# Bounds of query, key and value sizes: fewer TensorE instructions in a two-branch attention kernel

## The chip, the core and the metric

The kernel runs on one core of a Trainium2 chip. Five engines work side by side, each through its own queue in program order: TensorE (PE in the profile, with its weight loads as PEld), VectorE (DVE), ScalarE (ACT), GpSimd (POOL) and SyncE (SP, which issues the transfers). They wait for each other by semaphores. The metric is the time of one execution on the device in microseconds; lower is better. Before the change three runs took 1781.36, 1782.36 and 1781.55 us, median 1781.55.

## The reference

Two attention branches over 2048 positions and 1024 features with 32 heads of 32, their outputs side by side. Branch A works in four segments of 512 positions: inside a segment causal softmax attention, plus a memory of the segments before, mixed by a gate per head. Branch B is linear attention with learned feature maps (two softmaxes a head).

```python
for s in range(N):                      # branch A, N = 4 segments of L = 512
    qs, ks, vs = q[:, :, s], k[:, :, s], v[:, :, s]
    logits = jnp.einsum("bhqd,bhkd->bhqk", qs, ks) * scale + mask
    a_dot = jnp.einsum("bhqk,bhkd->bhqd", _softmax(logits, axis=-1), vs)
    pq = phi(qs)                        # phi(t) = t + 1 where t > 0, else exp(t)
    num = jnp.einsum("bhld,bhde->bhle", pq, M)
    den = jnp.einsum("bhld,bhd->bhl", pq, z)[..., None] + 1e-6
    outs.append(g * num / den + (1.0 - g) * a_dot)
    pk = phi(ks)
    M = M + jnp.einsum("bhld,bhle->bhde", pk, vs)
    z = z + jnp.einsum("bhld->bhd", pk)
# branch A returns o @ wo; branch B: softmax feature maps of q and k,
# kv = phi_k^T v, out = (phi_q kv) / (phi_q z) @ wo; the result is [a, b]
```

All arrays are float32.

## The kernel before

**Precision.** Large products run in float16 in two halves: a float32 matrix is scaled to a known size, rounded to a high half, and the rest becomes the low half; three matmuls (high-high, high-low, low-high) then make one product. The scaling needs a bound for each product's result, so that it too can be split into halves. A bound comes from two sums: for a segment x of the input, `xam[:, x]` holds per partition the largest absolute values, and for a block of weights `wgb[:, k, m]` (queries m = 0, keys m = 1 of group k) or `wvb[:, k]` (values) the sums of absolute values per partition. Their product summed over the 128 partitions bounds every entry of the projection.

**Work.** A group g (eight of them) is four heads, 128 columns of queries and of keys; values come in four blocks of two groups. The order of branch A is a list of 32 units, each one segment and one group: units 0 to 15 take segments 0 and 1 through all groups, units 16 to 31 segments 2 and 3. The index k of the bounds counts groups over both passes: k = 0 to 7 are the groups with segments 0 and 1, k = 8 to 15 the same groups with segments 2 and 3. For the values k = 0 to 3 and 4 to 7. `produce(u)` projects queries, keys and values of a unit, `attend(u)` does its attention, `values(u)` the value projection. `fold` and the `xpair` and `strassen` helpers belong to branch B, whose weights are prepared during branch A.

**The bounds.** `bounds(k, segs, prio)` (line 651) makes, for one group and one or two segments, a tile `bd` of five rows: scale and negative scale, inverse scale, the bound itself and the factor of the exponent. For each segment PE multiplies the column `xam[:, x]`, spread over 128 columns as the weights, with the group's two columns of `wgb` (line 659). DVE then scales and clamps the result (line 662), takes the reciprocal (664) and the exponent's factor (665), and POOL does three small products (667, 670, 671). `bounds_v(k, segs, prio)` (line 673) does the same for a block of values with one column (line 680), with lines 683, 685 and 687 on DVE and 689 on POOL; line 687 also keeps the largest bound of all values in `big`. Readers are `produce` (lines 721 to 734), `values` (700, 707) and `attend` (808, 810, 871).

**When they are called.** Groups 0 and 1 and value block 0 are called with one segment at a time, since segment 1 is loaded later. In the loop over units, every even unit u loads the weights of group u / 2 + 2 and calls its bounds with both segments; every fourth unit (u = 1, 5, ...) does so for the next block of values.

**Order.** Nothing is issued directly. `op(engine, duration, function, r=, w=, prio=)` records an operation with the tiles that it reads and writes, an assumed duration and a priority (twice the unit's number, plus an offset). `Graph.run` then hands out all operations by a simulation: at each step the engine that can start first takes, among those ready, the one with the lowest priority number; for PE those come first whose inputs are safe by a margin. Its choice is the program order of each engine. PSUM banks are given out in the same pass, by kind; the bounds use the kind "misc". Buffers with a tag rotate: a new one may be written when the readers of the one that many buffers before are done (`bd` has four, `bv` three).

Of the kernel before, what the change touches and what calls it, by code (L numbers as in the profile page):

```python
# [8 lines left out]
F32 = mybir.dt.float32  # L9
# [3 lines left out]
AF = mybir.ActivationFunctionType  # L13
# [230 lines left out]
def tile_kernel(ctx: ExitStack, tc: tile.TileContext, ax, aw, awv, awo, beta, bx, bwqk, bwv, bphi, bwo, out):  # L244
# [51 lines left out]
    big = const.tile([128, 2], F32, name="big")  # L296
    nc.vector.memset(big, 0.0)
    wsc = const.tile([128, 3, 2, 2], F32, name="wsc")
    osc2 = const.tile([128, 2, 2], F32, name="osc2")
# [287 lines left out]
    def group(u):  # L587
        return units[u][0] // 2 * NG + units[u][1]
# [7 lines left out]
    bigs, swfs, wscs, oscs, phss = (G.fixed(t) for t in (big, swf, wsc, osc2, phs))  # L596
    pstb, wmb = (G.fixed(t) for t in (pst, wm))
    osc = G.fixed(oa_d)
# [52 lines left out]
    def bounds(k, segs, prio):  # L651


        bd = bds.get(k) or bds.setdefault(k, G.buf("a", [128, 5, 2, 2], F32, "bd", 4))
        s0, n, kk = segs[0], len(segs), k % NG
        v, w = slice(s0 % 2, s0 % 2 + n), [(bd, x % 2) for x in segs]
        ps = bank("misc", [128, 2, 2], "bounds")
        for x in segs:
            op(PE, 0.14, lambda x=x: nc.tensor.matmul(
                ps()[:, x % 2], xam[:, x:x + 1].to_broadcast([128, 128]), wgb[:, kk], start=True, stop=True),  # L660
               r=[(xams, x), (wgbs, (kk, 0)), (wgbs, (kk, 1))], w=[ps], prio=prio)
        op(DVE, 0.1, lambda: nc.vector.tensor_scalar(bd()[:, 3, v], ps()[:, v], 2.0 ** -12, 1e-30, op0=OP.mult, op1=OP.max),
           r=[ps], w=w, prio=prio)
        op(DVE, 0.12, lambda: nc.vector.reciprocal(bd()[:, 2, v], bd()[:, 3, v]), w=w, prio=prio)
        op(DVE, 0.1, lambda: nc.vector.scalar_tensor_tensor(
            bd()[:, 4, v, 0], bd()[:, 3, v, 0], SCALE, bd()[:, 3, v, 1], op0=OP.mult, op1=OP.mult), w=w, prio=prio)
        op(POOL, 0.2, lambda: nc.gpsimd.tensor_tensor(
            bd()[:, 0, v], xsc[:, s0:s0 + n, 0:1].to_broadcast([128, n, 2]), wgs[:, kk, :, 0][:, None, :].to_broadcast([128, n, 2]), op=OP.mult),
           r=[*((xscs, x) for x in segs), (wgss, (kk, 0)), (wgss, (kk, 1))], w=w, prio=prio)
        op(POOL, 0.2, lambda: nc.gpsimd.tensor_tensor(bd()[:, 2, v], bd()[:, 2, v], bd()[:, 0, v], op=OP.mult), w=w, prio=prio)  # L670
        op(POOL, 0.2, lambda: nc.gpsimd.tensor_scalar(bd()[:, 1, v], bd()[:, 0, v], -1.0, None, op0=OP.mult), w=w, prio=prio)

    def bounds_v(k, segs, prio):

        bv = bvs.get(k) or bvs.setdefault(k, G.buf("a", [128, 3, 2], F32, "bv", 3))
        s0, n, kk = segs[0], len(segs), k % 4
        v, w = slice(s0 % 2, s0 % 2 + n), [(bv, x % 2) for x in segs]
        ps = bank("misc", [128, 2], "bounds")
        for x in segs:
            op(PE, 0.14, lambda x=x: nc.tensor.matmul(  # L680
                ps()[:, x % 2:x % 2 + 1], xam[:, x:x + 1].to_broadcast([128, 128]), wvb[:, kk:kk + 1], start=True, stop=True),
               r=[(xams, x), (wvbs, kk)], w=[ps], prio=prio)
# [3 lines left out]
        a, b = s0 % 2, (s0 + n - 1) % 2  # L686
        op(DVE, 0.1, lambda: nc.vector.scalar_tensor_tensor(
            big[:, 0:1], bv()[:, 1, a:a + 1], bv()[:, 1, b:b + 1], big[:, 0:1], op0=OP.max, op1=OP.max), r=w, w=[(bigs, 0)], prio=prio)
        op(POOL, 0.4, lambda: nc.gpsimd.tensor_scalar(bv()[:, 0, v], xsc[:, s0:s0 + n, 0], wvs[:, kk, 0:1], None, op0=OP.mult),
           r=[*((xscs, x) for x in segs), (wvss, kk)], w=w, prio=prio)  # L690

    def values(u):

        s, g = units[u]
        k = group(u) // 2
        w, x, P, d = wt[k, "v"], xt[s], 2 * u, un[u]
        d["bv"] = bv = bvs[k]
        i2, n0, vf = s % 2, 128 * (g % 2), vfb[u % 3]
        sc = d["sc"] = G.buf("a", [128, 4], F32, "sc", 4)
        op(POOL, 0.39, lambda: nc.gpsimd.tensor_scalar(sc(), gate1[:, 4 * g:4 * g + 4], bv()[:, 1, i2:i2 + 1], None, op0=OP.mult),  # L700
           r=[gates, (bv, i2)], w=[sc], prio=P + VPRIO)
# [5 lines left out]
        op(ACT, 0.62, lambda: nc.scalar.activation(vf()[:, :, 0:128], ps(), AF.Copy, scale=bv()[:, 0, i2:i2 + 1]),  # L707
           r=[ps, (bv, i2)], w=[vf], prio=P + VPRIO)

    def produce(u):  # L710
# [3 lines left out]
        d = un.setdefault(u, {})  # L714
        bd, i2, st = bds[k], s % 2, stk[u % 3]
        h3 = d["h3"] = G.buf("slot", [128, 2, 2, 512], F16, "h3", 2)
        for m in (1, 0):
            ps = bank("proj", [128, 512])
            product((ps, ps), lambda a, c: (w, (m, a, c // 4), lambda m=m: w()[:, m, a, c, :]), at(x), NC, P, dur=0.215)
            E = P  # L720
            op(ACT, 0.57, lambda ps=ps, m=m: nc.scalar.activation(h3()[:, m, 0], ps(), AF.Copy, scale=bd()[:, 2, i2, m:m + 1]),
               r=[ps, (bd, i2)], w=[(h3, (m, 0))], prio=E)
            op(DVE, 0.6, lambda ps=ps, m=m: nc.vector.scalar_tensor_tensor(
                h3()[:, m, 1], ps(), bd()[:, 2, i2, m:m + 1], h3()[:, m, 0], op0=OP.mult, op1=OP.subtract),
               r=[ps, (h3, (m, 0)), (bd, i2)], w=[(h3, (m, 1))], prio=E)
# [4 lines left out]
            if (m == 1 and s < NSEG - 1) or (m == 0 and s > 0):  # L730
                d[name] = p = G.buf("a", [128, 512], F32, name, 2)
                z = G.buf("a", [128, 512], F32, "z", 1)
                for o, i in ((z, 0), (p, 1)):
                    op(ACT, 0.59, lambda o=o, i=i, ps=ps, m=m: nc.scalar.activation(o(), ps(), AF.Relu, scale=bd()[:, i, i2, m:m + 1]),
                       r=[ps, (bd, i2)], w=[o], prio=E)
                op(ACT, 0.5, lambda p=p: nc.scalar.activation(p(), p(), AF.Exp, bias=0.0, scale=-1.0), w=[p], prio=E)
                op(POOL, 1.25, lambda p=p, z=z: nc.gpsimd.tensor_tensor(p(), p(), z(), op=OP.add), r=[z, p], w=[p], prio=E)
        values(u)

    def attend(u):  # L740
        s, g = units[u]
        d, P = un.pop(u), 2 * u + 1
        st, vl, vf, bd, bv, i2 = stk[u % 3], vlb[u % 2], vfb[u % 3], bds[group(u)], d["bv"], s % 2
        KR, QR = [(st, (1, r)) for r in range(3)], [(st, (0, r)) for r in range(3)]
# [60 lines left out]
        def v4(t):  # L805
            return t()[:, :, 0:128].rearrange("p c (h d) -> p c h d", d=32)

        act(0.52, lambda: nc.scalar.activation(vl()[:, :, :, 33:65], v4(vf), AF.Copy, scale=bv()[:, 2, i2:i2 + 1]),
            r=[vf, (bv, i2)], w=[(vl, 0)])
        dve(0.6, lambda: nc.vector.scalar_tensor_tensor(  # L810
            vl()[:, :, :, 0:32], v4(vf), bv()[:, 2, i2:i2 + 1], vl()[:, :, :, 33:65], op0=OP.mult, op1=OP.subtract),
            r=[vf, (bv, i2), (vl, 0)], w=[(vl, 1)], port=True)
# [43 lines left out]
        def scores(blocks, diag):  # L856
# [13 lines left out]
            pe(0.218, f, r=KR + QR + [(st, (1, 3))] + [(st, (0, 3 + h)) for h, _ in blocks], w=[ps])  # L870
            act(0.59, lambda: nc.scalar.activation(ps(), ps(), AF.Exp, bias=0.0, scale=bd()[:, 4, i2, 0:1]), r=[(bd, i2)], w=[ps])  # L871
            ph = G.buf("a", [128, 2, 512], F16, "ph", 6)
# [194 lines left out]
    for u in range(NU):  # L1067
# [19 lines left out]
        attend(u)  # L1087
# [485 lines left out]
```

## Time and profile before

| what | value |
|---|---|
| median of three runs | 1781.55 us (1781.36 to 1782.36) |
| span of the profiled execution, the only time that it has | 1779.5 us |
| instructions | 38925 |
| PE busy | 1715.4 us, 96% |
| weight loads busy | 1040.4 us, 58% |
| DVE busy | 1457.1 us, 82% |
| ACT busy | 1130.8 us, 64% |
| POOL busy | 922.3 us, 52% |
| matmul records of line 659 (queries and keys) | 64 |
| matmul records of line 680 (values) | 32 |
| granted TensorE clock, mean | 0.992 |

How to read it: the span is the time from the first to the last instruction on the profiled core, and "busy" sums the time in which an engine worked. A row of a line or tile gives the engine, the operation, what it writes `<-` what it reads, the shapes, and the durations in nanoseconds as least / median / most. A view of waits names who waited, for whom, the total in microseconds, how often and the longest. Matmuls overlap one another, so the duration of one record is longer than the time that it takes from the stream. Branch A, where the bounds are made, ends at about 920 us; what follows is branch B's second half and the output products.

### The profile page before, as it was taken

To read this page: it belongs to the slowest core of one execution; us is meant where nothing else is said; L and a number is where in the kernel's file an instruction comes from. 1 tells how busy PE (TensorE), PEld (TensorE's weight loads), DVE (VectorE), ACT (ScalarE), POOL (GpSimd) and SP (SyncE) were. 2 spreads that over 40 slices of the span, in tenths; PEclk is the share of its full clock that TensorE was granted. 3 is DMA by queue.
4 is the path that set the end of the run, shared out by engine and by line. 5 is a ranking of instruction groups with operands and counts; after the bars stand their busy time and mean duration, and the time that the engine had idled before them with its cause. 6 is when DMAs were issued, how large, how long until landed. Compare 5 with 4: busy or idle time off the path is not lost. (4 is left out here: it accounts for less than half of the span.)

```text
span 1779.5 us, 38925 instructions
## 1 busy us (share of the span) xinstructions
PE 1715.4 (96%) x14712; PEld 1040.4 (58%) x14712; DVE 1457.1 (82%) x3367; ACT 1130.8 (64%) x2095; POOL 922.3 (52%) x1141
## 2 busy tenths in 40 slices
PE   7999999999999999999989989999899999999999
PEld 5767766677776777677644444444555444554444
DVE  6989989899787888788877999988997888877541
ACT  6897886987866878689674756444644454344441
POOL 6445454555756687777583544433456677431000
PEclk9999999999999999999989999999999999999999
DMA  6546555574545453674565244276411333133311
GB/s 208 169 144 183 159 153 158 167 225 129 160 128 156 109 179 110 161 217 121 179 202 193 96 168 137 113 272 227 139 49 63 119 125 107 66 143 137 119 65 65
DMA packets 173260, 258.92 MB, mean 146 GB/s; under 512 B 69904, under 2 KB 122896, under 8 KB 164368
## 3 DMA queue, kind: packets, MB, share of 16 engines
q1 hardware_dynamic: 173072, 256.44, 44.9%
q8 instruction: 115, 1.88, 0.4%
q14 instruction: 73, 0.60, 0.1%
HBM read 145.44 MB, written 85.00 MB: 129 GB/s over the span
## 5 line engine op out<-in xcount | busy, mean ns | idle before, releaser
L359 PE MATMUL proj<-S,S 128*128 128x128 f16 (+1 forms) x3072 | 502.7, 299 | 5.5 <-ACT S L386 3.6
L359 PEld LDWEIGHTS <-S 128*128 128x128 f16 x4608 | 331.3, 99 | 153.6 <-issue 8.9
L549 PE MATMUL proj<-S,S 128*128 128x512 f16 x1488 | 348.7, 382 | 12.3 <-ACT cs L555 3.9
L549 PEld LDWEIGHTS <-S 128*128 128x128 f16 x1968 | 189.0, 99 | 231.3 <-issue 17.2
L880 POOL TENSOR_SCALAR_AFFINE_SELECT ph<-ph 128x256 f16<-128x256 f16 (+1 forms) x448 | 196.3, 460 | 171.8 <-DVE ph L874 134.9
L874 DVE SCALAR_TENSOR_TENSOR ph<-s,ph 128x512 f16<-128x512 f32 x320 | 210.4, 683 | 56.5 <-ACT ph L873 54.5
L775 DVE CUSTOM_DVE_ANT_0 s<-s,causal 128x512 f32<-128x512 f32 (+3 forms) x512 | 242.3, 510 | 12.0 <-PE s L769 8.4
L871 ACT ACTIVATE s<-s,bd 128x512 f32<-128x512 f32 x320 | 212.2, 710 | 21.8 <-PE s L867 21.4
L873 ACT ACTIVATE ph<-s 128x512 f16<-128x512 f32 x320 | 190.4, 656 | 0.6
L1119 ACT ACTIVATE e<-e,sk 128x256 f32<-128x256 f32 x256 | 113.9, 497 | 98.3 <-DVE e L1116 94.5
L359 PE MATMUL misc<-S,ot 128*128 128x512 f16 x768 | 174.1, 379 | 0.0
L1415 POOL TENSOR_TENSOR e<-e,zb 128x512 f32<-128x512 f32 x64 | 84.5, 1343 | 71.5 <-DVE r L1122 65.8
L359 PEld LDWEIGHTS <-ot 128*128 128x128 f16 x768 | 73.4, 98 | 82.1
L769 PE MATMUL s<-S 96*128 96x512 f16 (+3 forms) x512 | 113.3, 300 | 5.8 <-DVE mt L775 4.2
L867 PE MATMUL s<-S 104*128 104x512 f16 (+3 forms) x512 | 113.9, 300 | 1.5 <-DVE quad L1011 0.8
L359 PE MATMUL proj<-wv,S 128*128 128x128 f16 x1536 | 104.2, 221 | 0.3 <-DVE mt L775 0.3
L903 PEld LDWEIGHTS <-ph 128*128 128x128 f16 x2560 | 87.8, 96 | 18.0 <-POOL ph L880 2.0
L1226 POOL TENSOR_TENSOR e<-e,r 128x1024 f32<-128x1024 f32 x32 | 64.4, 2017 | 61.3 <-DVE r L1125 50.4
L903 PE MATMUL pv<-vl,ph 128*128 128x66 f16 (+1 forms) x2560 | 92.9, 185 | 2.2 <-POOL ph L880 1.6
L1122 DVE TENSOR_REDUCE r<-e 128x32 f32<-128x1024 f32 x64 | 76.7, 1205 | 21.6 <-ACT e L1119 21.6
L1428 POOL TENSOR_TENSOR e<-e,r 128x1024 f32<-128x1024 f32 x32 | 62.9, 1970 | 41.9 <-DVE r L1426 38.3
L549 PE MATMUL s<-S,S 128*128 128x512 f16 x324 | 77.1, 379 | 1.8 <-ACT cs L555 1.8
(302 smaller groups left out, 3334.8 us busy)
## 6 DMA issues: line engine op xcount, KB each, us to landing
S<-h SPq DMA_DIRECT2D x192, 128.0 KB
S<-wf_d SPq DMA_DIRECT2D x21, 1024.0 KB
st<-bwqk SPq DMA_DIRECT2D x64, 256.0 KB
wf_d<-fo SPq DMA_DIRECT2D x48, 256.0 KB
out<-os SPq DMA_DIRECT2D x40, 256.0 KB
wf_d<-oT SPq DMA_DIRECT2D x36, 256.0 KB
S<-xf_d SPq DMA_DIRECT2D x9, 1024.0 KB
S<-aw SPq DMA_DIRECT2D x16, 512.0 KB
```

Source lines behind the costliest of these rows:

```text
L359: op(PE, dur, lambda c=c, a=a, b=b, lv=lv, rv=rv: nc.tensor.matmul(pv(), lv(), rv(), start=(c == 0 and a + b == 0), stop=(c == n - 1 and a ...
L549: op(PE, 0.215, lambda n=n, a=a, b=b, lv=lv, rv=rv: nc.tensor.matmul(ps(), lv(), rv(), start=(start and n == 0 and a + b == 0), stop=(n == ...
L769: nc.tensor.matmul(ps()[:, o:o + 128 * i + 128], st()[0:96, 0, h, 128 * i:128 * i + 128], st()[0:96, 1, h, 0:128 * i + 128], start=True, s ...
L775: dve(0.12 + 0.00113 * n, lambda h=h, i=i, o=o, n=n: nc.vector.tensor_tensor_reduce(ps()[:, o:o + n], ps()[:, o:o + n], causal[:, 512 - n: ...
L867: nc.tensor.matmul(ps()[:, o:o + n], st()[0:104, 1, h, 128 * j:128 * j + 128], st()[0:104, 0, h, 128 * j:512], start=True, stop=True)
L871: act(0.59, lambda: nc.scalar.activation(ps(), ps(), AF.Exp, bias=0.0, scale=bd()[:, 4, i2, 0:1]), r=[(bd, i2)], w=[ps])
L873: act(0.5, lambda: nc.scalar.activation(ph()[:, 0], ps(), AF.Copy, scale=2.0 ** 14), r=[ps], w=[(ph, 0)])
L874: dve(0.6, lambda: nc.vector.scalar_tensor_tensor(ph()[:, 1], ps(), 2.0 ** 14, ph()[:, 0], op0=OP.mult, op1=OP.subtract), r=[ps, (ph, 0)], ...
L880: nc.gpsimd.affine_select(pd, pd, pattern=[[0, n], [1, 128]], compare_op=OP.is_ge, fill=0.0, base=0, channel_multiplier=-1)
L903: nc.tensor.matmul(ps()[:, i, n0:n1], ph()[:, a, o:o + 128], vl()[:, j, h, n0:n1], start=(i == 0 and a == 0), stop=(j == min(i, 2)), skip_ ...
L1119: op(ACT, 0.41, lambda i=i: nc.scalar.activation(e()[:, 4 * i:4 * i + 4], e()[:, 4 * i:4 * i + 4], AF.Exp, bias=0.0, scale=sk()[:, i:i + 1 ...
L1415: op(POOL, 1.35, lambda a=a, h0=h0, e=e: nc.gpsimd.tensor_tensor(e()[:, 8 * a:8 * a + 8], e()[:, 8 * a:8 * a + 8], zv()[:, h0:h0 + 8], op= ...
```

## The change

Three edits in `bounds` and `bounds_v`, and one where they are called.

1. For the second pass (k = 8 to 15, values 4 to 7) the bounds of all groups are made by one call, for k = 8 and k = 4. Each segment's matmul then has all columns of `wgb` (16) or `wvb` (4) on its right. One buffer of a new tag (`bdh`, `bvh`) holds them for the whole pass; calls for later k are dropped.
2. In the first pass, where both segments are asked for at once (groups 2 to 7, values 1 to 3), POOL first multiplies `xam` of the two segments with the group's columns into a small tile `pr`, and PE sums that over the partitions with one matmul, whose weights are the column of ones. This takes the place of two matmuls.
3. The rows of `bd` are four instead of five (the bound itself lies in row 1 until POOL overwrites it with the negative scale), the readers index through a small function, and the ring of `bv` has two buffers instead of three. The largest value bound of the second pass is taken by a reduction into a new tile `vmx` and a maximum with `big`, and line 689's product becomes one of two tensors.

The readers in `produce`, `values` and `attend` read the same numbers at new places. The core of the diff:

```diff
     def bounds(k, segs, prio):
-        bd = bds.get(k) or bds.setdefault(k, G.buf("a", [128, 5, 2, 2], F32, "bd", 4))
-        s0, n, kk = segs[0], len(segs), k % NG
-        v, w = slice(s0 % 2, s0 % 2 + n), [(bd, x % 2) for x in segs]
-        ps = bank("misc", [128, 2, 2], "bounds")
-        for x in segs:
-            op(PE, 0.14, lambda x=x: nc.tensor.matmul(
-                ps()[:, x % 2], xam[:, x:x + 1].to_broadcast([128, 128]), wgb[:, kk], start=True, stop=True),
-               r=[(xams, x), (wgbs, (kk, 0)), (wgbs, (kk, 1))], w=[ps], prio=prio)
+        rest = k >= NG
+        ks = slice(0, NG) if rest else slice(k % NG, k % NG + 1)
+        nk = NG if rest else 1
+        if k not in bds:
+            t = G.buf("a", [128, 4, 2, nk, 2], F32, "bdh" if rest else "bd", 1 if rest else 4)
+            for i in range(nk):
+                bds[k + i] = (t, lambda i=i: t()[:, :, :, i, :])
...
+        if n > 1 and not rest:
+            pr = G.buf("a", [128, 2, nk, 2], F32, "pr", 1)
+            op(POOL, 0.2, lambda: nc.gpsimd.tensor_tensor(
+                pr(), xam[:, s0:s0 + n, None, None].to_broadcast(shape), wgb[:, None, ks].to_broadcast(shape), op=OP.mult),
+               r=[(xams, x) for x in segs] + wg, w=[pr], prio=prio)
+            op(PE, 0.14, lambda: nc.tensor.matmul(ps(), one.to_broadcast([128, 128]), pr(), start=True, stop=True),
+               r=[pr], w=[ps], prio=prio)
+        else:
+            for x in segs:
+                op(PE, 0.14, lambda x=x: nc.tensor.matmul(
+                    ps()[:, x % 2], xam[:, x:x + 1].to_broadcast([128, 128]), wgb[:, ks], start=True, stop=True),
+                   r=[(xams, x)] + wg, w=[ps], prio=prio)
...
     def bounds_v(k, segs, prio):
-        bv = bvs.get(k) or bvs.setdefault(k, G.buf("a", [128, 3, 2], F32, "bv", 3))
+        rest = k >= 4
+        ks = slice(0, 4) if rest else slice(k % 4, k % 4 + 1)
+        nk = 4 if rest else 1
+        if k not in bvs:
+            t = G.buf("a", [128, 3, 2, nk], F32, "bvh" if rest else "bv", 1 if rest else 2)
...
+        if n > 1 and not rest:
+            pr = G.buf("a", [128, 2, nk, 1], F32, "pr", 1)
+            op(POOL, 0.2, lambda: nc.gpsimd.tensor_tensor(
+                pr()[:, :, :, 0], xam[:, s0:s0 + n, None].to_broadcast(shape), wvb[:, None, ks].to_broadcast(shape), op=OP.mult),
+               r=[(xams, x) for x in segs] + wv, w=[pr], prio=prio)
+            op(PE, 0.14, lambda: nc.tensor.matmul(ps(), one.to_broadcast([128, 128]), pr()[:, :, :, 0], start=True, stop=True),
+               r=[pr], w=[ps], prio=prio)
...
+        if rest:
+            op(DVE, 0.1, lambda: nc.vector.tensor_reduce(vmx, bv()[:, 1, v], axis=AX.XY, op=OP.max), r=w, w=[vmxs], prio=prio)
+            op(DVE, 0.1, lambda: nc.vector.tensor_tensor(big[:, 0:1], big[:, 0:1], vmx, op=OP.max), r=[vmxs], w=[(bigs, 0)], prio=prio)
...
-            x = 2 * ((u // 4 + 1) // 4)
-            bounds_v(u // 4 + 1, [x, x + 1], 2 * u + 0.5)
+            if u // 4 + 1 <= 4:
+                x = 2 * ((u // 4 + 1) // 4)
+                bounds_v(u // 4 + 1, [x, x + 1], 2 * u + 0.5)
...
-            x = 2 * ((k + 2) // NG)
-            bounds(k + 2, [x, x + 1], 2 * u + 3.5)
+            if k + 2 <= NG:
+                x = 2 * ((k + 2) // NG)
+                bounds(k + 2, [x, x + 1], 2 * u + 3.5)
```

More of the change, by code (lines that the diff above doesn't have):

```diff
@@ L297, in tile_kernel @@
     nc.vector.memset(big, 0.0)
+    vmx = const.tile([128, 1], F32, name="vmx")
     wsc = const.tile([128, 3, 2, 2], F32, name="wsc")
@@ L596, in tile_kernel @@
     bigs, swfs, wscs, oscs, phss = (G.fixed(t) for t in (big, swf, wsc, osc2, phs))
-    pstb, wmb = (G.fixed(t) for t in (pst, wm))
+    pstb, wmb, vmxs = (G.fixed(t) for t in (pst, wm, vmx))
     osc = G.fixed(oa_d)
@@ new lines, in bounds @@
+        v, w, shape = slice(s0 % 2, s0 % 2 + n), [(bd, x % 2) for x in segs], [128, n, nk, 2]
+        ps = bank("misc", [128, 2, nk, 2], "bounds")
+        wg = [(wgbs, (i, m)) for i in range(ks.start, ks.stop) for m in range(2)]
+        if n > 1 and not rest:
[10 more added lines that the diff above has]
+                   r=[(xams, x)] + wg, w=[ps], prio=prio)
@@ L667, in bounds @@
         op(POOL, 0.2, lambda: nc.gpsimd.tensor_tensor(
-            bd()[:, 0, v], xsc[:, s0:s0 + n, 0:1].to_broadcast([128, n, 2]), wgs[:, kk, :, 0][:, None, :].to_broadcast([128, n, 2]), op=OP.mult),
-           r=[*((xscs, x) for x in segs), (wgss, (kk, 0)), (wgss, (kk, 1))], w=w, prio=prio)
+            bd()[:, 0, v], xsc[:, s0:s0 + n, 0][:, :, None, None].to_broadcast(shape),
+            wgs[:, ks, :, 0][:, None].to_broadcast(shape), op=OP.mult),
+           r=[*((xscs, x) for x in segs), *((wgss, (i, m)) for i in range(ks.start, ks.stop) for m in range(2))], w=w, prio=prio)
@@ L673, in bounds_v @@
     def bounds_v(k, segs, prio):
-        bv = bvs.get(k) or bvs.setdefault(k, G.buf("a", [128, 3, 2], F32, "bv", 3))
[L676 to L682, printed above, removed]
+        rest = k >= 4
[3 more added lines that the diff above has]
+            t = G.buf("a", [128, 3, 2, nk], F32, "bvh" if rest else "bv", 1 if rest else 2)
+            for i in range(nk):
+                bvs[k + i] = (t, lambda i=i: t()[:, :, :, i])
+        bv = bvs[k][0]
+        s0, n = segs[0], len(segs)
+        v, w, shape = slice(s0 % 2, s0 % 2 + n), [(bv, x % 2) for x in segs], [128, n, nk]
+        ps = bank("misc", [128, 2, nk], "bounds")
+        wv = [(wvbs, i) for i in range(ks.start, ks.stop)]
+        if n > 1 and not rest:
[5 more added lines that the diff above has]
+               r=[pr], w=[ps], prio=prio)
+        else:
+            for x in segs:
+                op(PE, 0.14, lambda x=x: nc.tensor.matmul(
+                    ps()[:, x % 2], xam[:, x:x + 1].to_broadcast([128, 128]), wvb[:, ks], start=True, stop=True),
+                   r=[(xams, x)] + wv, w=[ps], prio=prio)
         op(DVE, 0.1, lambda: nc.vector.tensor_scalar(bv()[:, 1, v], ps()[:, v], 2.0 ** -15, 1e-30, op0=OP.mult, op1=OP.max),
@@ L685, in bounds_v @@
         op(DVE, 0.12, lambda: nc.vector.reciprocal(bv()[:, 2, v], bv()[:, 1, v]), w=w, prio=prio)
[L686 to L690, printed above, removed]
+        if rest:
+            op(DVE, 0.1, lambda: nc.vector.tensor_reduce(vmx, bv()[:, 1, v], axis=AX.XY, op=OP.max), r=w, w=[vmxs], prio=prio)
+            op(DVE, 0.1, lambda: nc.vector.tensor_tensor(big[:, 0:1], big[:, 0:1], vmx, op=OP.max), r=[vmxs], w=[(bigs, 0)], prio=prio)
+        else:
+            a, b = s0 % 2, (s0 + n - 1) % 2
+            op(DVE, 0.1, lambda: nc.vector.scalar_tensor_tensor(
+                big[:, 0:1], bv()[:, 1, a], bv()[:, 1, b], big[:, 0:1], op0=OP.max, op1=OP.max), r=w, w=[(bigs, 0)], prio=prio)
+        op(POOL, 0.4, lambda: nc.gpsimd.tensor_tensor(
+            bv()[:, 0, v], xsc[:, s0:s0 + n, 0][:, :, None].to_broadcast(shape), wvs[:, ks, 0][:, None].to_broadcast(shape), op=OP.mult),
+           r=[*((xscs, x) for x in segs), *((wvss, i) for i in range(ks.start, ks.stop))], w=w, prio=prio)
     def values(u):
```

30 lines of the change are left out of this document (16 added, 14 removed).

## The prediction

> **What bounds the kernel now.** I read the page of the profiled execution first: the busy shares, and the span in forty slices.
>
> ```profile
> span 1779.5 us, 38925 instructions
> PE 1715.4 (96%) x14712; PEld 1040.4 (58%) x14712; DVE 1457.1 (82%) x3367; ACT 1130.8 (64%) x2095; POOL 922.3 (52%) x1141
> PE   7999999999999999999989989999899999999999
> PEclk9999999999999999999989999999999999999999
> ```
>
> TensorE (PE) is busy 96% of the span at almost the full granted clock; VectorE (DVE) comes next with 82%. An average hides stages, so the next view is busy time by stretch (columns: length, then PE, weight loads, DVE, ACT, POOL with their counts, clock, DMA share, GB/s).
>
> ```profile
> 100.00:200.00 100.00, 98.83 (x1090) 71.27 (x1088) 90.28 (x234) 83.64 (x153) 52.45 (x84) 1.00 0.54 165
> 200.00:300.00 100.00, 94.87 (x989) 65.17 (x988) 90.14 (x259) 82.83 (x149) 47.70 (x80) 0.98 0.53 162
> 300.00:400.00 100.00, 97.00 (x1071) 70.91 (x1068) 88.75 (x243) 82.48 (x150) 51.32 (x86) 0.98 0.61 182
> 400.00:500.00 100.00, 99.56 (x1107) 71.06 (x1106) 84.70 (x258) 75.50 (x143) 63.34 (x106) 1.00 0.47 141
> 500.00:600.00 100.00, 100.00 (x1074) 70.13 (x1072) 79.10 (x246) 68.64 (x124) 61.76 (x90) 1.00 0.47 132
> 600.00:700.00 100.00, 99.79 (x1128) 71.56 (x1126) 86.23 (x234) 81.83 (x152) 75.19 (x114) 1.00 0.46 138
> 700.00:800.00 100.00, 99.25 (x1109) 71.01 (x1106) 81.08 (x248) 72.51 (x133) 73.71 (x107) 1.00 0.65 188
> 800.00:900.00 100.00, 97.90 (x1007) 65.92 (x1005) 82.30 (x235) 81.01 (x143) 69.39 (x102) 1.00 0.49 141
> ```
>
> All the work that the change touches lies between 57 and 768 us (rows below). There PE idles 1.17 + 5.13 + 3.00 = 9.3 us from 100 to 400 and 0.44 + 0 + 0.21 + 0.75 + 2.10 = 3.5 us from 400 to 900. Whatever leaves PE's stream there should shorten the stage by nearly its full length, since almost nothing waits for another engine.
>
> Third, the two lines whose matmuls go away, and how they stand in PE's stream (timeline of PE alone: start, length, engine, line, operation, tiles, count).
>
> ```profile
> L659 PE MATMUL misc<-wgb,xam x64: 165/251/251, 16.4 to 765.8; 128*128 128x2 f32 x64
> L680 PE MATMUL misc<-wvb,xam x32: 165/250/250, 27.7 to 711.9; 128*128 128x1 f32 x32
> 57.57 0.36 PE L370 MATMUL misc<-xam,one 128*128 128x1 f32 x2
> 57.84 0.56 PE L659 MATMUL misc<-wgb,xam 128*128 128x2 f32 x4
> 58.26 0.38 PE L359 MATMUL proj<-wv,S 128*128 128x128 f16 x4
> ...
> 71.87 0.38 PE L867 MATMUL s<-S 104*128 104x512 f16 x1
> 72.09 0.50 PE L659 MATMUL misc<-wgb,xam 128*128 128x2 f32 x4
> 72.46 0.38 PE L359 MATMUL proj<-S,S 128*128 128x512 f16 x1
> ...
> 507.25 0.34 PE L659 MATMUL misc<-wgb,xam 128*128 128x2 f32 x2
> 507.45 0.58 PE L680 MATMUL misc<-wvb,xam 128*128 128x1 f32 x4
> 507.89 0.36 PE L659 MATMUL misc<-wgb,xam 128*128 128x2 f32 x2
> 508.12 0.38 PE L359 MATMUL proj<-S,S 128*128 128x512 f16 x1
> ```
>
> Each float32 matmul of the program leaves two records: 32 products of line 659 are 64 records, 16 of line 680 are 32. The 250 ns of one record is not its cost, for they overlap; the cost is the distance to the next start. Two records span 0.36 us, one 0.25, so they start 0.11 us apart. A group of four takes 58.26 - 57.84 = 0.42 us behind narrow products and 72.46 - 72.09 = 0.37 behind a product 512 wide; eight in a row take 508.12 - 507.25 = 0.87.
>
> **The change part by part.** The sum is made on the profiled execution, whose only time is its span, 1779.5 us, 2.05 us under the median of the runs, 1781.55; I take the saving off the median.
>
> (1) Groups 8 to 15 of queries and keys: eight calls of two products become one call of two products, 16 columns wide. Seven calls, 28 records, leave PE. Most stand among narrow products at 0.42 us: 7 x 0.42 = 2.9 us. The remaining call keeps its four records. That 16 columns cost no more than 2 is bounded by a float32 product of 128 columns:
>
> ```profile
> 71.43 0.61 PE L1008 MATMUL misc<-phib,st 128*128 128x128 f32 x4
> L1008 PE MATMUL misc<-phib,st 128*128 128x128 f32 x256 | 36.1, 279 | 0.1
> L1125 DVE RECIPROCAL r<-r 128x32 f32<-128x32 f32 x64 | 21.3, 340 | 0.4
> ```
>
> Four of those span 0.61 us, one 0.28, so (0.61 - 0.28) / 3 = 0.11 us apart, as for 2 columns: nothing is added.
>
> (2) Values 4 to 7: four calls become one; three calls of four records go, 3 x 0.87 / 2 = 1.3 us.
>
> (3) Groups 2 to 7 and values 1 to 3: nine calls with both segments at once. Four records become two, the weights now the column of ones: 9 x 2 x 0.11 = 2.0 us. Single-segment calls (groups 0 and 1, value 0) keep theirs.
>
> Together 28 + 12 + 18 = 58 of 96 records and 2.9 + 1.3 + 2.0 = 6.2 us of PE's stream.
>
> (4) Added: nine small products on POOL, each ahead of PE's matmul, which now waits for POOL instead of for sizes that were long there. The nearest duration is line 667; the nearest wait is the one of the value products for the masked scores.
>
> ```profile
> L667 POOL TENSOR_TENSOR bd<-xsc,wgs x18: 188/200/650, 21.3 to 767.9; 128x4 f32<-128x4 f32 x14, 128x2 f32<-128x2 f32 x4
> L903 PE MATMUL pv<-vl,ph 128*128 128x66 f16 (+1 forms) x2560 | 92.9, 185 | 2.2 <-POOL ph L880 1.6 <-DVE mt L775 0.3 <-DVE ph L874 0.2
> PE pv L903 <- POOL ph L880: 1.6, 4, 0.9
> POOL ph L880 <- PE s L867: 7.9, 4, 4.2
> 87.12 0.65 POOL L667 TENSOR_TENSOR bd<-xsc,wgs 128x4 f32<-128x4 f32 x1
> ```
>
> Nine times 0.2 = 1.8 us of POOL, which is busy 52%. For PE: 2560 / 20 = 128 groups of value products stood behind POOL and lost 1.6 us, 0.0125 each; nine such waits make 0.1 us. The other end is nine times the longest, 0.9, or 8.1 us; below zero nothing speaks for a gain by the wait itself. I take 0.1, because the order puts a product where its inputs are expected, as it does for those 128. Behind a waiting matmul all of PE's stream queues, and then ACT and DVE, which read its banks.
>
> The row of line 667 also shows a spread of 188 to 650 ns. The Trainium skill, "GPSIMD Engine Reference", section "Key points", says that POOL shares its memory interfaces with DVE and contends with DVE instructions of two SBUF inputs; by its rule the added products would take the long end. The trace can't name the cause, but 9 x 0.65 = 5.9 us of POOL would still lie beside PE.
>
> (5) Removed on DVE and POOL, beside PE's work: seven calls' and three calls' worth of six and four small instructions.
>
> ```profile
> L662 DVE TENSOR_SCALAR bd<-misc x18: 145/159/164, 16.8 to 766.1; 128x4 f32<-128x4 f32 x14, 128x2 f32<-128x2 f32 x4
> L664 DVE RECIPROCAL bd<-bd x18: 147/167/178, 17.0 to 767.4; 128x4 f32<-128x4 f32 x14, 128x2 f32<-128x2 f32 x4
> L665 DVE SCALAR_TENSOR_TENSOR bd<-bd x18: 129/148/2053, 17.1 to 767.5; 128x2 f32<-128x2 f32 x14, 128x1 f32<-128x1 f32 x4
> L871 ACT ACTIVATE s<-s,bd x320: 623/690/958, 59.6 to 923.2; 128x512 f32<-128x512 f32 x160
> ```
>
> On DVE 7 x (0.159 + 0.167 + 0.148) = 3.3 us, and some 1.5 more for the values at like durations; the one call that does it all at once works on up to 32 elements, 0.34 us at most by line 1125 instead of 0.17. I cost and credit nothing: in these stretches PE does not wait for DVE beyond the few us above. POOL loses about 5 us and gains 1.8.
>
> (6) Lateness. The bounds of group k are made in unit 2k - 4 and first read in unit 2k. A unit lasts (923.2 - 59.6) / 32 = 27 us by line 871, so four units cover one more small step on POOL, even where POOL came to line 667 at 87.12, 15 us after the matmul at 72.09. The values' ring shrinks from three buffers to two: call k is made in unit 4k - 3 and takes the buffer last read in unit 4k - 5, two units earlier. Nothing waits. No DMA is added, removed or moved past another.
>
> Sum: -6.2 + 0.1 = -6.1 us, 1781.55 - 6.1 = 1775.4.
>
> **The rivals.** First, the order is drawn anew (not slower at its mild end, slower at its hard end). The order on all engines is written by a planner that picks by readiness and priority; from the first changed call, at 72 us, everything may be exchanged with its neighbours. For it: PE's idle share differs fourfold between stretches of the same loop, 9.3 us in 300 (3.1%) against 3.5 in 500 (0.7%), so 400 to 900 has more to lose than to gain. If it idled like 100 to 400, 500 x 9.3 / 300 = 15.5 us, that is 12 more and 1775.4 + 12 = 1787.4. Against: the units around are the same, with fewer small steps between. It ends on the slow side from 6.1 + 3.6 = 9.7 us of new idle time; with half of 12 it gives 1781.4, no change. It may also gain: half of the 9.3 us closed gives 1770.8.
>
> Second, the records were nearly free. Behind the 512-wide product the first of the four costs 0.37 - 3 x 0.11 = 0.04 us, its weight load hidden. Were all so, 58 x 0.04 = 2.3 us, 1779.2, within what a measurement can tell. Against it stand the rows with 0.11 and the 0.87 for eight. The Trainium skill, "TensorE: Matmul & The Clock Gate", section "Back-to-back issue gap", gives 1 to 64 columns about 60 cycles, some 25 ns, as the gap of an isolated matmul; by that an estimate of 58 x 25 ns = 1.5 us, 1780.1. The trace disagrees for float32 records that follow each other, 0.11 us.
>
> Third, PE stands behind POOL. POOL's in-order queue holds masks that themselves wait for score products (4.2 us at the longest). If the nine waits cost the mean of those, 7.9 / 4 = 2.0 each, 18 us are lost and the time is 1781.55 - 6.2 + 18 = 1793; it is slower from 9.8 / 9 = 1.1 us a wait, more than the longest wait of PE for POOL seen, 0.9.
>
> **How the numbers follow.** A run tells about 0.2% from no change, 3.6 us. The saving lands, with small losses or gains of order: 0.60, own range 1770 to 1778. No change: 0.22, of which order 0.18 and free records 0.04. Slower: 0.18, order 0.15 and POOL 0.03. So 0.60, 0.22, 0.18. The range takes in the gaining order at 1770.8, a little more below, and most of the losing one: 1769.5 to 1786, leaving out about one in ten on each side.
>
> **What would show it.** Lines 659 and 680's successors with 24 and 14 records; PE's busy time some 6 us lower, its idle time before 900 us still near 13 us after the first 100; unit starts after 400 us earlier by steps of 0.4; waits of PE on the new product under 1 us in sum. Wrong: PE's idle time up by more than 4 us in 100 to 900 or after 900, a new row "PE misc" waiting for POOL "pr" with a microsecond or more, or PE's busy time down by 2 us only.

## The result, and the profile after

Four runs of the changed kernel took 1773.0 to 1774.87 us, median 1773.51; four of the kernel before took a median of 1781.95 us. The ratio is 0.9941 with a 95% interval from 0.9928 to 0.9953, which is 10.5 us (8.4 to 12.8); the medians lie 8.4 us apart, at the near end of it. The forecast was 1775.4 us, in a range of 1769.5 to 1786.0, and faster as the likeliest case. The profiled execution of the changed kernel spans 1771.4 us against 1779.5.

The page of the changed kernel, busy shares and the granted clock in forty slices:

```profile
span 1771.4 us, 38769 instructions
PE 1711.7 (97%) x14654; PEld 1036.3 (58%) x14654; DVE 1454.1 (82%) x3338; ACT 1133.2 (64%) x2095; POOL 921.8 (52%) x1126
PEclk9999999999999999999989999999999999999999
```

PE has 14712 - 14654 = 58 records fewer, as counted. Its busy time fell by 1715.4 - 1711.7 = 3.7 us only; the other 4.4 us of the span are idle time that went. The two executions differ in the granted clock too, 0.992 before and 0.988 after: 0.004 x 1775 = 7 us of clock were withheld in addition, which by an estimate can hide up to as much of the busy time that the records saved. Busy time by stretch says where (columns as in the prediction: length, PE, weight loads, DVE, ACT, POOL, clock, DMA share, GB/s):

```profile
100.00:200.00 100.00, 100.00 (x1113) 72.37 (x1112) 90.48 (x248) 85.54 (x156) 51.18 (x85) 1.00 0.56 163
200.00:300.00 100.00, 96.99 (x1032) 70.01 (x1029) 94.19 (x263) 86.27 (x155) 51.58 (x87) 0.98 0.58 172
300.00:400.00 100.00, 99.17 (x1083) 70.17 (x1083) 84.85 (x235) 81.95 (x148) 50.14 (x92) 1.00 0.58 174
400.00:500.00 100.00, 98.97 (x1138) 72.15 (x1135) 90.22 (x257) 77.01 (x143) 64.02 (x98) 1.00 0.55 163
500.00:600.00 100.00, 100.00 (x1125) 70.94 (x1124) 83.78 (x239) 79.23 (x145) 71.75 (x101) 1.00 0.51 145
600.00:700.00 100.00, 98.98 (x1115) 69.81 (x1114) 83.20 (x247) 76.42 (x139) 67.31 (x98) 1.00 0.39 120
700.00:800.00 100.00, 98.92 (x1046) 68.77 (x1045) 84.00 (x250) 76.62 (x141) 74.90 (x101) 1.00 0.63 194
800.00:900.00 100.00, 97.92 (x956) 64.41 (x954) 79.99 (x218) 75.01 (x132) 74.00 (x102) 0.97 0.51 146
```

From 100 to 400 us PE idles 0 + 3.01 + 0.83 = 3.8 us where it idled 9.3; from 400 to 900 it idles 5.2 us where it idled 3.5. The sum of the prediction has no term for the 5.5 us that went from 100 to 400: the change removes work from PE, not waits. From 800 to 900 the clock is 0.97 where it was 1.00.

The products for the bounds, by line, in the changed kernel (least / median / most ns, first and last start):

```profile
L669 POOL TENSOR_TENSOR pr<-xam,wgb x6: 196/201/645, 57.1 to 360.4; 128x4 f32<-128x4 f32 x6
L707 POOL TENSOR_TENSOR pr<-xam,wvb x3: 197/197/198, 99.6 to 335.1; 128x2 f32<-128x2 f32 x3
L672 PE MATMUL misc<-pr,one x12: 167/252/272, 72.4 to 362.0; 128*128 128x4 f32 x12
L676 PE MATMUL misc<-wgb,xam x12: 182/251/263, 16.4 to 380.2; 128*128 128x2 f32 x8, 128*128 128x16 f32 x4
L710 PE MATMUL misc<-pr,one x6: 166/251/251, 101.1 to 337.0; 128*128 128x2 f32 x6
L714 PE MATMUL misc<-wvb,xam x8: 167/250/253, 28.0 to 380.8; 128*128 128x1 f32 x4, 128*128 128x4 f32 x4
```

PE's stream around two of them, a timeline of PE alone in the same kernel:

```profile
72.41 0.28 PE L672 MATMUL misc<-pr,one 128*128 128x4 f32 x2
72.55 0.59 PE L360 MATMUL proj<-S,S 128*128 128x512 f16 x2
...
380.15 0.34 PE L676 MATMUL misc<-wgb,xam 128*128 128x16 f32 x2
380.35 0.38 PE L360 MATMUL proj<-S,S 128*128 128x512 f16 x1
```

Lines 672 and 676 hold 24 records, 710 and 714 hold 14, 38 of the former 96. The bounds of group 2 now take 72.55 - 72.41 = 0.14 us of the stream, where four records took 0.37. Two records 16 columns wide take 380.35 - 380.15 = 0.20 us, no more than two of 2 columns took before (507.25 to 507.45). No row of waits names PE as waiting for the product on POOL. The last exponential of branch A, line 910 now, starts earlier by 923.2 - 908.8 = 14.4 us, while the whole span is 8.1 us shorter:

```profile
L910 ACT ACTIVATE s<-s,bdh x160: 640/695/847, 499.0 to 908.8; 128x512 f32<-128x512 f32 x160
```

### The profile page after: what moved, and what is told of

It is laid out like the page before. It is cut to its first block, busy times and chain, and to the rows that moved or that the text cites. A ratio compares the mean times of both kernels' runs of the same rounds, so it can differ in the third digit from the quotient of the medians.

```text
span 1771.4 us, 38769 instructions
## 1 busy us (share of the span) xinstructions
PE 1711.7 (97%) x14654; PEld 1036.3 (58%) x14654; DVE 1454.1 (82%) x3338; ACT 1133.2 (64%) x2095; POOL 921.8 (52%) x1126
## 5 line engine op out<-in xcount | busy, mean ns | idle before, releaser
L550 PE MATMUL proj<-S,S 128*128 128x512 f16 x1488 | 348.9, 383 | 12.8 <-ACT cs L556 6.9
L814 DVE CUSTOM_DVE_ANT_0 s<-s,causal 128x256 f32<-128x256 f32 (+3 forms) x512 | 242.8, 508 | 9.2 <-PE s L808 3.9
L910 ACT ACTIVATE s<-s,bdh 128x512 f32<-128x512 f32 x160 | 106.0, 706 | 17.8 <-PE s L906 17.0
L910 ACT ACTIVATE s<-s,bd 128x512 f32<-128x512 f32 x160 | 107.1, 715 | 13.0 <-PE s L906 7.3
```

Of the source, the lines that this page charges most:

```text
L550: op(PE, 0.215, lambda n=n, a=a, b=b, lv=lv, rv=rv: nc.tensor.matmul(ps(), lv(), rv(), start=(start and n == 0 and a + b == 0), stop=(n == ...
L814: dve(0.12 + 0.00113 * n, lambda h=h, i=i, o=o, n=n: nc.vector.tensor_tensor_reduce(ps()[:, o:o + n], ps()[:, o:o + n], causal[:, 512 - n: ...
```

## The experiments

All comparisons are with the kernel before on the same chip; its median there was between 1783.7 and 1785.3 us. An interval of a ratio is some 0.1% to either side, about 2 us.

### What the records cost, with the order of the work kept

In the kernel before, with the order of the work kept on every engine, one product serves both segments and the second is not issued (shown for `bounds`; `bounds_v` has the same edit):

```diff
+        left = [False, True]
         for x in segs:
-            op(PE, 0.14, lambda x=x: nc.tensor.matmul(
-                ps()[:, x % 2], xam[:, x:x + 1].to_broadcast([128, 128]), wgb[:, kk], start=True, stop=True),
+            op(PE, 0.14, lambda x=x: (nc.tensor.matmul(
+                ps()[:, x % 2], xam[:, x:x + 1].to_broadcast([128, 128]), wgb[:, kk], start=True, stop=True) if n == 1 else
+                nc.tensor.matmul(ps(), xam[:, s0:s0 + 1].to_broadcast([128, 128]),
+                                 wgb[:, kk][:, None, :].to_broadcast([128, 2, 2]), start=True, stop=True) if left.pop() else None),
```

> The kernel before with its order kept on every engine: where both segments are asked for, only one of the two products is issued (to all columns, with the first segment's sizes, so the second segment is scaled by the first one's bound), and the second is left out. 21 products, 42 records, leave PE and nothing else moves. Theory A, a record costs its distance of 0.11 us: 42 x 0.11 = 4.6 us less than before, near 1777.3. Rival B, the order drawn anew made the gain and records are nearly free: 42 x 0.04 = 1.7 us or less, near 1780.3. Rival C, the small DVE and POOL steps that went made it: no change here, since they all stay.

Measured: 1778.63 us, ratio 0.9970 (0.9959 to 0.9982), that is 5.4 us less (3.2 to 7.3) for 42 records. On its page PE's busy time is 1715.4 - 1711.4 = 4.0 us lower, at the same clock of 0.992:

```profile
PE 1711.4 (96%) x14670; PEld 1035.3 (58%) x14670; DVE 1455.7 (82%) x3367; ACT 1131.4 (64%) x2095; POOL 923.0 (52%) x1141
```

The opposite, in the changed kernel with its order kept: the taken records are issued again in place (shown for `bounds`; `bounds_v` has the same edit).

```diff
-            op(PE, 0.14, lambda: nc.tensor.matmul(ps(), one.to_broadcast([128, 128]), pr(), start=True, stop=True),
+            op(PE, 0.14, lambda: [nc.tensor.matmul(ps(), one.to_broadcast([128, 128]), pr(), start=True, stop=True) for _ in range(2)],
...
-                op(PE, 0.14, lambda x=x: nc.tensor.matmul(
+                op(PE, 0.14, lambda x=x: [nc.tensor.matmul(
-                    ps()[:, x % 2], xam[:, x:x + 1].to_broadcast([128, 128]), wgb[:, ks], start=True, stop=True),
+                    ps()[:, x % 2], xam[:, x:x + 1].to_broadcast([128, 128]), wgb[:, ks], start=True, stop=True) for _ in range(nk)],
```

> The changed kernel with its order kept, and every taken record put back in place: the product with ones is issued twice, the second pass's products of queries and keys eight times and those of values four times, 29 products or 58 records more. Theory A: 58 x 0.11 = 6.4 us above the changed kernel, near 1779.9, some 2 us under the kernel before; these 2 us are then what the new order and the steps gone from DVE and POOL are worth. Rival B: little above the changed kernel, 1774 to 1776. Rival C: as B, since the DVE and POOL steps stay away.

Measured: 1780.42 us, ratio 0.9984 (0.9975 to 0.9993). Against the changed kernel's 0.9941 the 58 records cost 0.0043 x 1783 = 7.7 us (some 5 to 10, with the intervals of both ratios). The page of the changed kernel with the records put back:

```profile
span 1780.4 us, 38886 instructions
PE 1720.8 (97%) x14712; PEld 1044.1 (59%) x14712; DVE 1454.1 (82%) x3338; ACT 1133.3 (64%) x2095; POOL 920.7 (52%) x1126
```

In the two profiled executions, both at a clock of 0.988, all of it is PE's busy time: 1720.8 - 1711.7 = 9.1 us, and the span grew by 9.0. Both runs agree with theory A, 5.4 against 4.6 expected and 7.7 against 6.4; over both it is 13.1 / 100 = 0.13 us a record, and the interval of the first, 0.08 to 0.17, holds the 0.11 read from the trace. Rival B (records nearly free) falls, and rival C (only the DVE and POOL steps count) falls as the whole cause. What is left under the kernel before with all records back, 1 - 0.9984 = 2.9 us (1.2 to 4.5), is the worth of the new order and of the steps gone from DVE and POOL together; these two were not told apart.

### One half of the change at a time

The second pass alone: the changed kernel, in which both conditions for the product on POOL are switched off.

```diff
-        if n > 1 and not rest:
+        if False:
```

> The changed kernel without the product on POOL: in the first pass two products on PE as before, in the second one call for all groups. 40 records fewer than before, on PE 40 x 0.11 = 4.4 us. Theory A with a new order worth about what it was in the full change: 1775 to 1778. Rival B, order decides: anything from 1770 to 1786, not in step with the records. Rival C, the DVE and POOL steps that go (all of them go here) bring the gain: 1773 to 1775, as the full change.

The first pass alone: no call for all groups (shown for `bounds`; `bounds_v` has the same edit). Both halves keep the other parts of the change, the four rows of `bd` and the ring of two for `bv`.

```diff
-        rest = k >= NG
+        rest, later = False, k >= NG
...
-        if n > 1 and not rest:
+        if n > 1 and not later:
...
-            if k + 2 <= NG:
+            if True:
```

> The kernel before with the product on POOL and one product on PE in the first pass alone; the second pass makes its bounds call by call, with two products each. 18 records fewer than before, 18 x 0.11 = 2.0 us. Theory A with an order effect of a few us: 1778 to 1781. Rival B: anything from 1770 to 1786. Rival C: no gain, as no DVE step goes and POOL has nine more: 1781 to 1783. The sum of the losses of this one and of the second pass alone against the full change's 8.4 us tells how far the parts add up.

Measured: the second pass alone, with 40 records fewer, 1783.97 us, ratio 1.0005 (0.9996 to 1.0014): no gain. The first pass alone, with 18 fewer, 1771.76 us, ratio 0.9931 (0.9919 to 0.9944): as fast as the whole change. The parts go against the count of the records. With the cost measured above (0.13 us each) the second half saved some 5 us on PE and lost as much elsewhere, and the first saved 2.3 and gained some 10 elsewhere. Both expectations of theory A with a mild effect of order missed, and so did rival C for both; only "order decides" held. The pages, the second pass alone and then the first alone:

```profile
PE 1716.8 (96%) x14672; PEld 1038.6 (58%) x14672; DVE 1450.9 (81%) x3338; ACT 1133.6 (64%) x2095; POOL 916.3 (51%) x1117
PE 1709.4 (97%) x14694; PEld 1037.3 (59%) x14694; DVE 1453.4 (82%) x3367; ACT 1131.8 (64%) x2095; POOL 923.5 (52%) x1150
```

The second pass alone has 40 records fewer than before and yet 1.4 us more of PE's busy time. The granted clock differs: 0.9876 in the mean of its runs, 0.9934 in those of the first pass alone, 0.9899 in those of before. By an estimate the second half had 0.0023 x 1784 = 4.1 us of clock withheld more than before and the first 0.0035 x 1772 = 6.2 less, so a good part of what the halves lost and gained elsewhere is clock and not idle time. Busy time by stretch of the second pass alone, and then of the first alone:

```profile
100.00:400.00 300.00, 290.54 (x3140) 206.95 (x3139) 269.20 (x735) 248.22 (x448) 150.50 (x249) 0.99 0.56 169
400.00:900.00 500.00, 496.27 (x5417) 348.33 (x5416) 415.42 (x1209) 384.16 (x697) 341.05 (x496) 0.99 0.51 149
900.00:1400.00 500.00, 467.29 (x3143) 236.58 (x3142) 432.52 (x739) 267.47 (x543) 241.32 (x194) 0.98 0.43 152
```

```profile
100.00:400.00 300.00, 296.01 (x3254) 212.17 (x3253) 269.83 (x743) 254.84 (x460) 152.37 (x265) 1.00 0.58 170
400.00:900.00 500.00, 492.62 (x5354) 345.39 (x5353) 414.87 (x1216) 377.49 (x687) 349.31 (x518) 1.00 0.52 151
900.00:1400.00 500.00, 469.71 (x3165) 238.23 (x3163) 442.88 (x764) 272.60 (x556) 245.96 (x193) 0.98 0.43 152
```

From 100 to 400 us the second pass alone idles 9.5 us, as the kernel before, and the first pass alone 4.0, as the changed kernel: the better stretch came in with the first half. (Up to 380 us the order of the second pass alone is that of the kernel before, and the order of the first pass alone that of the changed kernel, so these are two orders there and not four.) Two explanations were open: the product on POOL brings a better order of itself (S), or the order is a draw and this draw was lucky (L).

### The order drawn anew, with the work unchanged

One number in the plan is changed, the duration assumed for the bounds' products (at each place where they are recorded); the instructions stay the same and only their order differs.

```diff
-            op(PE, 0.14, lambda x=x: nc.tensor.matmul(
+            op(PE, 0.22, lambda x=x: nc.tensor.matmul(
...
```

> The kernel before, same work, same instructions; only the duration that the planner assumes for the bounds' products is 0.22 us (what two records take in the trace) instead of 0.14, so the order is drawn anew. Theory L, the order is a draw and small changes of the plan move the time by several us either way: some time from 1774 to 1790, and idle time of PE from 100 to 400 us anywhere from 3 to 12 us. Theory S, the product on POOL itself gives the better order there: near 1783.7 (within 3 us), idle time from 100 to 400 about 9 us as before.

> As the last, with 0.10 us assumed: a third draw of the order for the work of before. Theory L: the three kernels of the same work lie several us apart. Theory S: all three within 3 us of 1783.7, with about 9 us of idle time from 100 to 400.

> The changed kernel with 0.22 us assumed for the bounds' products: same work, order drawn anew. Theory L: 1768 to 1784, idle time from 100 to 400 anywhere from 3 to 12 us. Theory S: within 3 us of the changed kernel, 1772 to 1777, idle time there near 4 us.

> The kernel with the product on POOL in the first pass alone, with 0.22 us assumed. Theory L: 1766 to 1786. Theory S: within 3 us of 1771.8, idle time from 100 to 400 near 4 us.

After these four a rule seemed possible, that a shorter assumed duration gives the better order, and three more were run on it, with the same edit.

> The changed kernel with 0.10 us assumed for the bounds' products: another draw of the order. Theory M, a shorter assumed duration gives the better order (all three families so far: 0.22 slower than 0.14, and 0.10 faster than 0.14 for the kernel before): 1765 to 1772. Theory L, a draw without a rule: anywhere from 1766 to 1786.

> The kernel with the product on POOL in the first pass alone, 0.10 us assumed. Theory M: under 1771.8, some 1762 to 1770. Theory L: anywhere from 1766 to 1790.

> The kernel before with 0.18 us assumed. Theory M: between the 1784 of 0.14 and the 1799.5 of 0.22, near 1792. Theory L: anywhere from 1772 to 1800.

Measured, as ratios to the kernel before (intervals of 0.001 to 0.0015 to either side), with the rows above set in:

| work (products for the bounds) | 0.10 us assumed | 0.14 | 0.18 | 0.22 |
|---|---|---|---|---|
| before (48) | 0.9941 | 1 | 0.9968 | 1.0084 |
| first pass alone (39) | 1.0012 | 0.9931 | | 1.0025 |
| second pass alone (28) | | 1.0005 | | |
| changed (19) | 0.9962 | 0.9941 | | 0.9974 |

The work of before, unchanged, ran at 1775.37 and at 1799.51 us, a spread of 0.0143, some 25 us. That is three to four times what the records are worth. Theory M falls: 0.10 is not the best in two of three rows, and 0.18 beats 0.14. Theory S falls too as a rule for the whole time: the first pass alone lies on both sides of 1. Its narrower form stays open: from 100 to 400 us the six kernels with the product on POOL at its planned length idle 3.1 to 4.1 us (three orders, since two kernels with the same assumed duration share theirs up to 380 us), and the four orders without it 9.3, 9.0, 7.0 and 3.4. That the fourth does as well without the product speaks for a draw; three against four don't settle it. Two draws of the same work, first with 0.22 and then with 0.10:

```profile
100.00:400.00 300.00, 291.00 (x3196) 208.53 (x3194) 267.76 (x754) 252.73 (x454) 150.47 (x259) 0.99 0.55 163
400.00:900.00 500.00, 492.12 (x5354) 347.10 (x5352) 409.65 (x1183) 374.60 (x679) 331.94 (x501) 0.99 0.52 150
900.00:1400.00 500.00, 459.98 (x3137) 234.03 (x3136) 439.91 (x772) 269.74 (x545) 251.99 (x200) 0.98 0.42 148
```

```profile
100.00:400.00 300.00, 296.62 (x3229) 212.25 (x3227) 262.18 (x747) 249.25 (x449) 147.76 (x254) 1.00 0.57 171
400.00:900.00 500.00, 494.00 (x5403) 347.34 (x5401) 424.65 (x1232) 383.09 (x696) 355.61 (x524) 1.00 0.51 150
900.00:1400.00 500.00, 469.11 (x3174) 237.92 (x3173) 441.76 (x754) 273.01 (x556) 243.45 (x193) 0.99 0.43 153
```

The slow draw idles 9.0, 7.9 and 40.0 us in the three stretches, the fast one 3.4, 6.0 and 30.9. The largest part of the idle time lies after 900 us, where branch A hands over to branch B and no bound is made any more. (The profiled execution of the fast draw is the fastest of its five, 4.5 us under their median.) Idle time is not all: the spans, 1796.5 and 1769.2 us, differ by 27.3 us, of which 1717.3 - 1710.5 = 6.8 are busy time of the same instructions, at clocks of 0.987 and 0.993. Over the runs the clock of the draws of before falls from 0.992 at 0.10 us assumed to 0.986 at 0.22, and that of the first pass alone from 0.993 at 0.14 to 0.987 at 0.22, with the time rising; in the changed kernel, 0.988 to 0.990, it does not go with the time. What sets it in each order was not followed.

```profile
PE 1717.3 (96%) x14712; PEld 1041.3 (58%) x14712; DVE 1462.0 (81%) x3367; ACT 1135.1 (63%) x2095; POOL 924.2 (51%) x1141
PE 1710.5 (97%) x14712; PEld 1039.0 (59%) x14712; DVE 1450.7 (82%) x3367; ACT 1133.8 (64%) x2095; POOL 922.1 (52%) x1141
```

No run beat the changed kernel clearly: the first pass alone (0.9931) and the kernel before with 0.10 (0.9941) are level with it.

### PE made to stand behind POOL

In the changed kernel with its order kept, the nine products on POOL are issued eleven times each (shown for `bounds`; `bounds_v` has the same edit).

```diff
-            op(POOL, 0.2, lambda: nc.gpsimd.tensor_tensor(
-                pr(), xam[:, s0:s0 + n, None, None].to_broadcast(shape), wgb[:, None, ks].to_broadcast(shape), op=OP.mult),
+            op(POOL, 0.2, lambda: [nc.gpsimd.tensor_tensor(
+                pr(), xam[:, s0:s0 + n, None, None].to_broadcast(shape), wgb[:, None, ks].to_broadcast(shape), op=OP.mult) for _ in range(11)],
```

> The changed kernel with its order kept, and each of the nine products on POOL issued eleven times in place, so that PE's product comes free some 10 x 0.2 = 2.0 us later in POOL's queue. If PE stands behind POOL (the third rival of the prediction), nine times up to 2 us are lost: up to 18 us above the changed kernel. If POOL's step lies well ahead of PE's need, as the trace's missing rows of waits on this tile say: within 3 us of the changed kernel, and any wait of PE for this tile is a row of its own.

Measured: 1784.94 us, ratio 1.0012 (1.0003 to 1.0021): against the changed kernel's 0.9941 a loss of 0.0071 x 1783 = 12.7 us. The waits of PE for the product in that run (total us, times, longest):

```profile
PE misc L672 <- POOL pr L669: 6.0, 4, 2.1
PE misc L710 <- POOL pr L707: 3.7, 3, 1.3
```

Its busy shares on the page:

```profile
PE 1715.8 (96%) x14654; PEld 1035.5 (58%) x14654; DVE 1454.5 (82%) x3338; ACT 1133.7 (64%) x2095; POOL 938.8 (53%) x1216
```

One of the waits and what follows, in the timeline of PE, and after it the busy time in stretches of 4 us (with the prediction's columns):

```profile
129.13 0.39 PE L672 MATMUL misc<-pr,one 128*128 128x4 f32 x2 [2.12 <-POOL pr L669]
131.02 0.63 PE L360 MATMUL proj<-S,S 128*128 128x512 f16 x1
```

```profile
126.00:130.00 4.00, 1.88 (x12) 0.95 (x10) 1.39 (x7) 3.02 (x6) 2.44 (x13) 1.00 0.41 98
130.00:134.00 4.00, 4.00 (x13) 1.62 (x12) 2.47 (x4) 2.73 (x5) 2.09 (x6) 0.57 0.02 4
134.00:138.00 4.00, 4.00 (x69) 2.99 (x67) 2.10 (x5) 3.45 (x8) 2.31 (x5) 1.00 0.29 65
```

Seven of the nine products wait, 9.7 us in all: POOL's lead over PE in the changed kernel is under 2 us in most places. In the profiled executions the span grew by 1784.6 - 1771.4 = 13.2 us: 9.1 are idle time, and 1715.8 - 1711.7 = 4.1 are busy time of the same instructions on PE.

## Why the prediction was right

- **PE's stream bounds branch A, and a record costs 0.11 us.** Right. With the order fixed, 42 records gave 5.4 us (3.2 to 7.3, or 4.4 to 10 for 58) and 58 took 7.7 (some 5 to 10); the sum of 6.2 lies within both. The second rival, records nearly free (1779.2 in all), is excluded: 42 of its records at 0.04 would have given 1.7 us, and 3.2 is the least that the interval allows.
- **16 columns cost no more than 2.** Right, 0.20 us for two records either way.
- **The wait for POOL at 0.1 us.** Right, no such wait is seen. But the cover is thin: 2 us later on POOL and PE waits seven times. The third rival named a real mechanism. At its threshold, 1.1 us a wait, it expected 3.6 us (0.2%) over the kernel before; at 9.7 / 9 = 1.1 us a wait the kernel is 0.12% slower. That the two lie so near is partly luck: 9.7 us of waits cost 12.7, but they came off a gain of 10.5 and not of 6.1.
- **Removed DVE and POOL steps worth nothing.** Not refuted: the second pass alone takes all of them away and gains nothing. They were not measured apart from the order.
- **The order.** This is the term that failed. The sum gave it nothing, and its signs to look for said that PE's busy time would fall by some 6 us and its idle time before 900 would stay near 13; measured were 3.7 us, and 3.8 + 5.2 = 9.0. Starts after 400 us were to come earlier by steps of 0.4; the last exponential came 14.4 us earlier, and behind branch A 14.4 - 8.1 = 6.3 us of that were lost again. The first rival priced a bad draw at +12 us, which was the right size (the worst was +0.0084, 15 us); a good draw was priced at 4.7 us, half of the idle time from 100 to 400, and that was too little: the best draw of the kernel before was 10.5 us better. Within the same work the ratios of the table scatter by 0.005 (the standard deviation, pooled over the three rows with several draws), 9 us. So the likeliest case's own range, 1770 to 1778, was far too narrow, and the whole range, 1769.5 to 1786, was too narrow on both sides: the best and the worst draw of before, set on 1775.4, give 1764.9 and 1790.4. Whether the chance of 0.18 for slower was right, these draws can't say: of the ten kernels beside the one before, three are slower by more than their interval, one with the work of before and two with nine products fewer, but none of the three with the full change.
- **So the forecast was met by the sum of a sound term and a mild draw, and the draw was luck.** The time lies in the range, but the saving that was forecast, 6.1 us, lies outside the measured interval of 8.4 to 12.8. Put by the runs, the records are worth 7.7 us and order and small steps 2.9; that these make up the measured 10.5 holds by construction, as both are read from the same two ratios. From the other run alone the 58 records are 58 x 5.4 / 42 = 7.5. With a draw like the 0.22 of the kernel before (+15 us) the same saving would, by this sum, have ended slower; that was not run.

Over the draws the work shows through: the mean of the four ratios of before is 0.9998, of the three of the changed kernel 0.9959. The difference, 0.0039 or 7 us, agrees with the records' worth, but seven draws with such a spread do not show it by themselves; the two runs with a fixed order do.

## What to carry to other kernels

Where a program hands out the order of all engines from assumed durations, any edit draws the order anew, and that draw can be worth several times the edit: here 25 us between orders of the same instructions against 6 to 8 us saved. Measure what an edit is worth with the order held (leave the instructions out, or issue them again, where they stand in the order), and judge a version by several orders, not one. A transfer of work from the engine that sets the time to another is safe only by the lead that the other has at that place, which one run with that work made longer tells.

## What was not expected

A short wait of PE cost more than itself. In the last experiment a wait of 2.12 us ends at 129.13; from 130 to 134 us the granted clock is 0.57, so 0.43 x 4 = 1.7 us are withheld, and a 512-wide product takes 0.63 us, where it takes 0.38 otherwise; at 134 the clock is full again. The changed kernel, with the same order and no wait there, keeps its clock:

```profile
126.00:130.00 4.00, 4.00 (x40) 2.24 (x39) 2.92 (x5) 4.00 (x9) 2.22 (x7) 1.00 0.36 78
130.00:134.00 4.00, 4.00 (x80) 3.51 (x79) 3.16 (x7) 4.00 (x9) 3.03 (x6) 1.00 0.29 66
```

Two more waits of that run, of 1.77 and 1.33 us, are followed by a low clock (0.60 from 266 to 270 us, 0.57 from 376 to 380); the other four, of 1.35, 1.22, 1.13 and 0.8 us, are not. That goes with the 4.1 us of longer products beside 9.0 us of new idle time from 100 to 400 us (12.8 against 3.8). The Trainium skill, "TensorE: Matmul & The Clock Gate", section "HAM oscillation — how this bites in real kernels", warns of idle gaps over some 3.4 us; here gaps of 1.3 to 2.1 us were enough, and the measurement decides. The length of one gap does not decide alone: in the changed kernel a longer one, 2.65 us, leaves the clock at 1.00 from 952 to 964 us.

```profile
957.70 0.60 PE L550 MATMUL proj<-S,S 128*128 128x512 f16 x2 [2.65 <-ACT S L387]
956.00:960.00 4.00, 2.29 (x10) 0.83 (x11) 4.00 (x8) 4.00 (x11) 0.80 (x1) 1.00 0.01 2
```

What else decides was not tried. Orders of the same instructions can so differ in busy time and not only in idle time, as the two draws above do.
